# Wide broadcast of inverse denominators, small layernorm steps and an early x in a fused attention and feed-forward kernel

## The chip, the cores and the metric

The kernel runs on one core of one Trainium2 chip. The metric is the device time of one execution in microseconds (us). A run is called fast here unless it is over 1.5% above the fastest run of the same kernel; ratios use fast runs alone. Names of the engines in the profile: PE is the matrix engine, ACT the scalar engine, DVE the vector engine, POOL the general one, and SP the one that does nothing here but issue transfers. "SPq" and "ACTq" in a row mean that this engine's sequencer was busy issuing a transfer.

## The reference

```python
xn = layernorm(x)                                # x: [1, 2048, 448] bf16
# attention with a memory: 16 heads of 28, 4 segments of 512 tokens
for s in range(4):
    p     = softmax(qs @ ks.T * scale + mask)    # causal, inside the segment
    a_dot = p @ vs
    num   = phi(qs) @ M                          # M, z: what earlier segments left
    den   = phi(qs) @ z + 1e-6
    o     = g * num / den + (1 - g) * a_dot      # g = sigmoid(beta), per head
    M, z  = M + phi(ks).T @ vs, z + sum(phi(ks))
s_ = concat(o) @ wo
gate = silu((gelu(xn @ w_gate) * (xn @ w_up)) @ w_down)   # 448 -> 1792 -> 448
out = x + s_ * gate
```

## The kernel before

The heads lie in four groups (g) of four. Everything is written in program order by a scheduler of its own: attention of a segment has 24 half-steps, n0 to n23, and each half-step issues one pair of scores, its exp on ACT, its causal mask on POOL (`affine_select`), the value products of two steps earlier, and then some "filler": projections, the down product, output blocks. In the traces each engine takes up its work in program order.

Both divisions, by the softmax denominator (side 0) and by the memory denominator (side 1), take one path: a row of each head's denominators is stored to DRAM, loaded back as [128, 64], inverted by DVE, stored again, and read back in four broadcasts, one for each head group, in which the row of each of its four heads goes to 32 partitions:

```python
def evac(s, g, side, ps):
    t = oup.tile([P, L], F32, name=f"oU{side}")          # pool of 4 buffers per side
    nc.vector.tensor_copy(out=t[:], in_=ps[:])
    oU[s, g, side] = t
    nc.sync.dma_start(out=den[s][side, g * HG:(g + 1) * HG, :], in_=t[Dh:P:HP, :])

def invert(s, side):
    dc = small.tile([P, 64], F32, name="dc")
    rdr = dram.tile([H, L], F32, name="rdr")
    nc.sync.dma_start(out=dc[:], in_=den[s][side].rearrange("h (c f) -> (h c) f", f=64))
    def rest():
        ...                                              # add, gate, reciprocal on DVE
        nc.sync.dma_start(out=rdr[:].rearrange("h (c f) -> (h c) f", f=64), in_=dc[:])
        for g in range(G):
            r = rbp.tile([P, L], F32, name="rb")
            nc.sync.dma_start(
                out=r[:], in_=rdr[g * HG:(g + 1) * HG, :].unsqueeze(1).to_broadcast([HG, HP, L]))
            rb[s, g, side] = r
    later(2, rest)                                       # two half-steps later

def combine(s, g):                                       # POOL
    ...
    nc.gpsimd.tensor_tensor(out=o_a[:], in0=o_a[:], in1=r[:], op=ALU.mult)
    nc.gpsimd.tensor_tensor(out=dst, in0=o_a[:], in1=oU.pop((s, g, 1))[:], op=ALU.add)
```

An output block (four per segment) loads its x once more as `xr`, multiplies, adds on POOL and stores. The load and the store both go through SP:

```python
def fin(b):
    xr = work.tile([P, D], BF16, name="xr")
    nc.sync.dma_start(out=xr[:], in_=x_v[s][:, b, :])
    ...                                                  # oT @ wo on PE, times the gate on DVE
    nc.gpsimd.tensor_tensor(out=o_out[:], in0=t[:], in1=xr[:], op=ALU.add)
    nc.sync.dma_start(out=o_v[s][:, b, :], in_=o_out[:])
```

At the start SP loads x, ACT loads wq; POOL squares wq and wk for a guard (a check that no logit can overflow), and DVE normalizes x.

Of the kernel before, what the change touches and what calls it, by code (L numbers as in the profile page):

```python
# [17 lines left out]
P = 128  # L18
NSEG = 4
HP = 32  # L20
# [5 lines left out]
def fast_path(tc, A_x, A_wq, A_wk, A_wv, A_wo, A_beta, B_w_gate, B_w_up, B_w_down, out):  # L26
# [16 lines left out]
    with ExitStack() as ctx:  # L43
# [25 lines left out]
        def load_x(s):  # L69
            x_sb[s] = xp.tile([P, NB, D], BF16, name="x_sb")  # L70
            for b in range(0, NB, 2):
                nc.sync.dma_start(out=x_sb[s][:, b:b + 2, :], in_=x_v[s][:, b:b + 2, :])

# [7 lines left out]

        wq_raw = seg1.tile([DC, NDC, D], BF16, name="hT")
        wk_raw = const.tile([DC, NDC, D], BF16, name="wk_raw")
# [4 lines left out]
        wo_sb = const.tile([P, G, D], BF16, name="wo_sb")  # L88
        w_dma(nc.scalar, wq_raw, A_wq, DC)
        w_dma(nc.scalar, wk_raw, A_wk, DC)  # L90
# [52 lines left out]
        def tick():  # L143
# [3 lines left out]
            for _, _, fn in due:  # L147
                fn()

        def guard():  # L150
            sqs = {}
            for nm in ("wq", "wk"):
                t = oup.tile([DC, NDC, D], BF16, name="oU" + ("0" if nm == "wq" else "1"))
                nc.gpsimd.tensor_tensor(out=t[:], in0=raw[nm][:], in1=raw[nm][:], op=ALU.mult)
                sqs[nm] = t
            ones = const.tile([P, 1], BF16, name="ones")
            nc.gpsimd.memset(ones[:], 1.0)
            nrm = small.tile([1, 2, H], F32, name="nrm")
            for i, nm in enumerate(("wq", "wk")):
                np_ = ps_m.tile([P, L], F32, name="m")  # L160
                for c in range(NDC):
                    nc.tensor.matmul(out=np_[0:1, 0:D], lhsT=ones[0:DC, :], rhs=sqs[nm][:, c, :],
                                     start=(c == 0), stop=(c == NDC - 1))
                nc.vector.reduce_sum(out=nrm[:, i, :],
                                     in_=np_[0:1, 0:D].rearrange("p (h d) -> p h d", d=Dh), axis=AX.X)
# [3 lines left out]
                                    scalar2=None, op0=ALU.is_lt)  # L169
            oki = const.tile([1, 1], mybir.dt.int32, name="oki")  # L170
            nc.vector.tensor_reduce(out=oki[:], in_=okh[:], op=ALU.min, axis=AX.X)
            return oki

        xnT = {}

        def layer_norm(s):
# [6 lines left out]

            def stats(h):
                for b in (h, h + 1):
                    st = small.tile([P, nc.vector.BN_STATS_DIM], F32, name="st")
                    nc.vector.bn_stats(out=st[:], in_=xs[:, b, :])
                    nc.vector.bn_aggr(out=mv[:, b, :], in_=st[:])
                r = rstd[:, h:h + 2]
                nc.vector.tensor_scalar(out=r, in0=mv[:, h:h + 2, 1], scalar1=EPS, scalar2=None,  # L190
                                        op0=ALU.add)
                nc.gpsimd.tensor_tensor(out=r, in0=r, in1=nhalf[:, h:h + 2], op=ALU.pow)  # L192

# [16 lines left out]

            def both(*fs):
                def run():
                    for f in fs:
                        f()
                return run
            A = lambda f, *a: (lambda: f(*a))
            return [A(stats, 0), A(stats, 2), A(scale_x, 0),
                    both(A(turn, 0), A(scale_x, 1)), both(A(put, 0), A(turn, 1), A(scale_x, 2)),
                    both(A(put, 1), A(turn, 2), A(scale_x, 3)), both(A(put, 2), A(turn, 3)), A(put, 3)]

# [128 lines left out]
        def memory_read(s, g):  # L349
            np_ = ps_m.tile([P, L], F32, name="m")  # L350
            nc.tensor.matmul(out=np_[:], lhsT=mbd[:, g, :], rhs=pqT[s][:, g, :], start=True, stop=True)
            evac(s, g, 1, np_)

        rb = {}

        def invert(s, side):

            dc = small.tile([P, 64], F32, name="dc")
            rdr = dram.tile([H, L], F32, name="rdr")
            nc.sync.dma_start(out=dc[:], in_=den[s][side].rearrange("h (c f) -> (h c) f", f=64))  # L360

            def rest():
                nc.vector.tensor_scalar(out=dc[:], in0=dc[:], scalar1=(1e-6 if side else 0.0),
                                        scalar2=igate[:, side:side + 1], op0=ALU.add, op1=ALU.mult)
                nc.vector.reciprocal(out=dc[:], in_=dc[:])
                nc.sync.dma_start(out=rdr[:].rearrange("h (c f) -> (h c) f", f=64), in_=dc[:])
                for g in range(G):
                    r = rbp.tile([P, L], F32, name="rb")
                    nc.sync.dma_start(
                        out=r[:], in_=rdr[g * HG:(g + 1) * HG, :].unsqueeze(1).to_broadcast([HG, HP, L]))  # L370
                    rb[s, g, side] = r
            later(2, rest)

# [123 lines left out]

        with tc.manual_schedule():
            ln = layer_norm(0)
            ln[0]()  # L500
            pad_weight("wq")
            for f in ln[1:]:
                f()
            pad_weight("wk")
            gates()
            run(project_units(0))
            oki = guard()

            for s in range(NSEG):
                last = s == NSEG - 1  # L510

                if not last:
                    table = {}
                    if s > 0:
                        p_ = s - 1
                        in_turn(table, 0, ends)
                        in_turn(table, 2, [lambda: invert(p_, 0)])
                        in_turn(table, 9, [lambda g=g: combine(p_, g) for g in range(G)])
                    in_turn(table, 1, layer_norm(s + 1))
                    gate_up(s, table)  # L520
                if s + 2 < NSEG:
                    load_x(s + 2)
# [3 lines left out]
                if last:  # L526
                    in_turn(at, 0, ends)
                    in_turn(at, 2, [lambda: invert(s - 1, 0)])
                    in_turn(at, 8, [lambda g=g: combine(s - 1, g) for g in range(G)])
                    in_turn(at, 13, [lambda g=g: memory_read(s, g) for g in range(G)])  # L530
                    in_turn(at, 18, [lambda: invert(s, 1)])
                elif s > 0:
                    pre += [(0.22, lambda g=g: memory_read(s, g)) for g in range(G)]
                    in_turn(at, 7, [lambda s=s: invert(s, 1)])
                    in_turn(at, 14, [lambda s=s, g=g: scale_memory(s, g) for g in range(G)], 2)
                if not last:
                    pre.append((0.9, lambda s=s: update(s)))
                    lists.append(project_units(s + 1))
                if s < 2:
                    lists.append(down_units(s))  # L540
                if last:
                    lists.append(down_units(s - 1))
                    pre += merge(*lists)
                    lists = [finish_units(s - 1)]
                elif s > 0:
                    lists.append(finish_units(s - 1))
                ends = attention(s, pre + merge(*lists), at)
# [3 lines left out]
            in_turn(table, 0, ends)  # L551
            in_turn(table, 3, [lambda g=g: scale_memory(s, g) for g in range(G)])
            in_turn(table, 2, [lambda: invert(s, 0)])
# [389 lines left out]
```

## Time and profile before

| | before |
|---|---|
| median of the first three runs | 360.02 us (358.03 to 363.34) |
| span of the profile, granted clock of PE | 359.6 us, 0.916 |
| first projection on PE | 17.5 us |
| holes of PE over 2 us after that | 9.9, 13.0, 5.7, 13.1, 2.9 us |

The page's busy times (us, share of the span, number of instructions):

```profile
PE 281.8 (78%) x1619; PEld 115.5 (32%) x1620; DVE 162.5 (45%) x301; ACT 149.5 (42%) x211; POOL 139.5 (39%) x221
```

A hole is a stretch in which PE runs no matmul. PE has 78 us without work, and no other engine is half busy. So the question is not which engine has too much work, but what PE waits for at each hole, followed back. The granted clock is the share of full speed that PE was given; when it is 0.5, the texts call the clock cold or half. "Segment 1" in the prediction is attention 1 here, and so on.

### The profile page before, as it was taken

Reading aid. Unit: us, or ns where it says so; the run is one execution under the profiler, and the core shown is the slowest. Engines: PE = TensorE matmul, PEld = TensorE weight load, DVE = VectorE, ACT = ScalarE, POOL = GpSimd, SP = SyncE. Lnnn points to the kernel's source line nnn. Section 1 sums busy time; section 2 is a strip of 40 time slices with the busy share of each in tenths; the row PEclk is TensorE's granted clock in tenths of the full one; section 3 lists DMA queues with packets and bytes.
Section 4 is the critical chain, followed back from the end, with each engine's and each line's share of the span. In section 5 each row is a group of like instructions: output and inputs, shape, how many; then the busy total and the mean of one; then the engine's idle time right before and its main releaser. Section 6 shows DMA issues by size and latency. Waiting matters only on the chain. (4 is left out here: it accounts for less than half of the span.)

```text
span 359.6 us, 4459 instructions
## 1 busy us (share of the span) xinstructions
PE 281.8 (78%) x1619; PEld 115.5 (32%) x1620; DVE 162.5 (45%) x301; ACT 149.5 (42%) x211; POOL 139.5 (39%) x221
## 2 busy tenths in 40 slices
PE   0299999999999989908998988509875960599991
PEld 0234344333334433302343433102331320134450
DVE  2748754555566475602558556503311540034341
ACT  1223323866742375611652367504681750013310
POOL 6620100433310454106621567018648720452822
PEclk9999999999999999965999999856996996579998
DMA  7996000000001400121000201121112023102111
GB/s 189 262 289 130 0 1 2 0 5 1 3 5 42 129 19 16 42 93 39 9 21 9 102 20 29 59 77 39 30 39 86 7 57 106 52 17 83 52 51 48
DMA packets 17414, 20.32 MB, mean 57 GB/s; under 512 B 3064, under 2 KB 12792, under 8 KB 17384
## 3 DMA queue, kind: packets, MB, share of 16 engines
q1 hardware_dynamic: 15960, 17.55, 16.7%
q10 hardware_dynamic: 1392, 2.41, 2.6%
q8 instruction: 14, 0.23, 0.3%
q14 instruction: 16, 0.13, 0.1%
q0 software_dynamic: 32, 0.00, 0.0%
HBM read 17.66 MB, written 2.29 MB: 56 GB/s over the span
## 5 line engine op out<-in xcount | busy, mean ns | idle before, releaser
L322 ACT ACTIVATE pt<-s 128x1024 bf16<-128x1024 f32 (+1 forms) x96 | 82.3, 884 | 61.2 <-PE s L318 35.0
L325 POOL TENSOR_SCALAR_AFFINE_SELECT pt<-pt 128x256 bf16<-128x256 bf16 x128 | 51.5, 423 | 68.4 <-ACT pt L322 67.9
L400 ACT ACTIVATE gl<-s 128x512 bf16<-128x512 f32 x56 | 33.4, 597 | 91.4 <-PE s L397 87.3
L401 DVE TENSOR_TENSOR hT<-gl,s 128x512 bf16<-128x512 bf16 x56 | 38.4, 685 | 66.7 <-ACT gl L400 66.7
L397 PE MATMUL s<-xnT,wg_sb 112*128 112x512 bf16 x224 | 59.8, 391 | 1.2 <-DVE hT L401 1.2
L397 PE MATMUL s<-xnT,wu_sb 112*128 112x512 bf16 x224 | 59.3, 389 | 0.0
L335 PE MATMUL pv<-pt,vaug 128*32 128x512 bf16 (+3 forms) x256 | 21.1, 326 | 46.6 <-POOL pt L325 40.3
L412 PE MATMUL m<-wd_sb,hT 128*128 128x448 bf16 x224 | 51.6, 367 | 0.0
L441 POOL TENSOR_TENSOR o_out<-sg,xr 128x448 bf16<-128x448 f32 x16 | 16.5, 1031 | 65.6 <-DMA xr<-in_A_x_dram 47.5
L318 PE MATMUL s<-qT,kT 32*128 32x128 bf16 (+3 forms) x256 | 33.1, 311 | 2.5 <-ACT pt L322 1.8
L397 PEld LDWEIGHTS <-wu_sb 112*128 112x128 bf16 x224 | 22.3, 100 | 27.7 <-issue 2.2
L397 PEld LDWEIGHTS <-wg_sb 112*128 112x128 bf16 x224 | 21.2, 100 | 26.1 <-issue 5.3
L345 DVE COPY oU<-pv 128x512 f32<-128x512 f32 x16 | 10.9, 684 | 37.2 <-PE pv L335 28.3
L412 PEld LDWEIGHTS <-hT 128*128 128x128 bf16 x224 | 20.3, 100 | 22.3 <-issue 6.5
L335 PEld LDWEIGHTS <-vaug 128*32 128x32 bf16 x256 | 6.3, 95 | 59.7 <-issue 57.3
L192 POOL TENSOR_TENSOR rstd<-rstd,nhalf 128x2 f32<-128x2 f32 x8 | 5.9, 742 | 45.3 <-DVE rstd L190 45.3
L385 POOL TENSOR_TENSOR oU<-oU,rb 128x512 f32<-128x512 f32 x12 | 15.2, 1266 | 20.6 <-DMA rb<-rdr 20.2
L318 PEld LDWEIGHTS <-kT 32*128 32x128 bf16 x256 | 9.9, 92 | 37.4 <-issue 37.1
L202 PE MATMUL m<-ident,xn 128*112 128x128 bf16 x64 | 7.1, 249 | 17.0 <-DVE xn L196 16.7
L234 PE MATMUL m<-xnT,wq_pad 112*128 112x512 bf16 x64 | 18.3, 412 | 0.7 <-ACT xnT L207 0.7
L234 PE MATMUL m<-xnT,wk_pad 112*128 112x512 bf16 x64 | 18.4, 415 | 0.0
L421 DVE SCALAR_TENSOR_TENSOR sg<-th,m 128x448 f32<-128x448 f32 x16 | 9.8, 614 | 15.4 <-ACT th L416 13.3
(75 smaller groups left out, 289.7 us busy)
## 6 DMA issues: line engine op xcount, KB each, us to landing
rb<-rdr SPq DMA_DIRECT2D x28, 256.0 KB
x_sb<-in_A_x_dram SPq DMA_DIRECT2D x8, 224.0 KB
xr<-in_A_x_dram SPq DMA_DIRECT2D x16, 112.0 KB
out_dram<-o_out SPq DMA_DIRECT2D x16, 112.0 KB
wu_sb<-in_B_w_up_dram ACTq DMA_DIRECT2D x1, 1568.0 KB
wg_sb<-in_B_w_gate_dram SPq DMA_DIRECT2D x1, 1568.0 KB
wd_sb<-in_B_w_down_dram SPq DMA_DIRECT2D x1, 1568.0 KB
den<-oU SPq DMA_DIRECT2D x28, 8.0 KB
```

The lines of the kernel that those rows point to most:

```text
L234: nc.tensor.matmul(out=pr[:], lhsT=wpad[nm][:, c, g * HG:(g + 1) * HG, :].rearrange("p h d -> p (h d)"), rhs=xnT[s][:, c, :], start=(c == ...
L318: nc.tensor.matmul(out=sp[:, j, c0:c0 + n], lhsT=kT[s][r, g, kb * P:(kb + 1) * P], rhs=qT[s][r, g, kb * P:L], start=True, stop=True)
L322: nc.scalar.activation(out=pt[:, :, 0:w], in_=sp[:, :, 0:w], func=ACT.Exp, scale=scale)
L325: nc.gpsimd.affine_select(out=v, in_=v, pattern=[[0, 2], [1, P]], compare_op=ALU.is_ge, fill=0.0, base=0, channel_multiplier=-1)
L335: nc.tensor.matmul(out=acc[i * HP:(i + 1) * HP, kb * P:L], lhsT=va[:, kb, g * HG + i, :], rhs=pts[i // 2][:, i % 2, c0:c0 + n], start=(kb ...
L345: nc.vector.tensor_copy(out=t[:], in_=ps[:])
L385: nc.gpsimd.tensor_tensor(out=o_a[:], in0=o_a[:], in1=r[:], op=ALU.mult)
L397: nc.tensor.matmul(out=gu[:, i, :], lhsT=w_sb[:, c, fc * P:(fc + 1) * P], rhs=xnT[s][:, c, :], start=(c == 0), stop=(c == NDC - 1))
L400: nc.scalar.activation(out=gl[:], in_=gu[:, 0, :], func=ACT.Gelu_apprx_tanh)
L401: nc.vector.tensor_tensor(out=hT[s][:, fc, :], in0=gl[:], in1=gu[:, 1, :], op=ALU.mult)
L412: nc.tensor.matmul(out=d_ps[:, 0:D], lhsT=hT[s][:, fc, b * P:(b + 1) * P], rhs=wd_sb[:, fc, :], start=(fc == 0), stop=(fc == NFC - 1))
L441: nc.gpsimd.tensor_tensor(out=o_out[:], in0=t[:], in1=xr[:], op=ALU.add)
```

## The change

Its intent: the broadcast reads a source whose slowest dimension is 16 and not four, and is meant to go over 16 transfer engines; `xr`, which comes behind it, should land early. For this the inverse is written four times. Besides, layernorm is spread over more steps of gate/up, the guard's squares go from POOL to ACT, x is loaded first over both queues, and the memory reads, scalings and output blocks are laid out anew. The core of it, cut:

```diff
-                nc.sync.dma_start(out=x_sb[s][:, b:b + 2, :], in_=x_v[s][:, b:b + 2, :])
+                eng = nc.scalar if s == 0 and b else nc.sync
+                eng.dma_start(out=x_sb[s][:, b:b + 2, :], in_=x_v[s][:, b:b + 2, :])
...
-        w_dma(nc.scalar, wq_raw, A_wq, DC)
+        w_dma(nc.sync, wq_raw, A_wq, DC)
...
-                nc.gpsimd.tensor_tensor(out=t[:], in0=raw[nm][:], in1=raw[nm][:], op=ALU.mult)
+                nc.scalar.activation(out=sqs[nm][:], in_=raw[nm][:], func=ACT.Square)
...
+            if g == G - 1:                               # in memory_read
+                later(2, lambda: invert(s, 1))
+                for i in range(G):
+                    later(11 + 2 * i, lambda i=i: scale_memory(s, i))
...
-            rdr = dram.tile([H, L], F32, name="rdr")
+            rdr = dram.tile([H, 4, L], F32, name="rdr")
-                nc.sync.dma_start(out=rdr[:].rearrange("h (c f) -> (h c) f", f=64), in_=dc[:])
+                for j in range(4):
+                    nc.sync.dma_start(out=rdr[:, j, :].rearrange("h (c f) -> h c f", f=64), in_=dc[:])
-                        out=r[:], in_=rdr[g * HG:(g + 1) * HG, :].unsqueeze(1).to_broadcast([HG, HP, L]))
+                        out=r[:], in_=rdr[g * HG:(g + 1) * HG].rearrange("h j l -> (h j) l")
+                        .unsqueeze(1).to_broadcast([HG * 4, HP // 4, L]))
-            later(2, rest)
+            later(3, rest)
...
-                    in_turn(at, 8, [lambda g=g: combine(s - 1, g) for g in range(G)])
-                    in_turn(at, 13, [lambda g=g: memory_read(s, g) for g in range(G)])
-                    in_turn(at, 18, [lambda: invert(s, 1)])
+                    in_turn(at, 10, [lambda g=g: combine(s - 1, g) for g in range(G)])
+                    in_turn(at, 15, [lambda g=g: memory_read(s, g) for g in range(G)])
```

(Left out: the table of 16 small layernorm steps in place of eight, the order of layernorm 0 around the two weight copies, the guard as two steps inside gate/up 0, and a reordering of the filler.)

## The prediction

> **What bounds the kernel now.** I read the page's row of slices first, then the list of waits, then the timelines of PE, POOL and of the SP queue around each hole in PE, and last the first 20 us.
>
> The page's slices, 9 us each:
>
> ```profile
> PE   0299999999999989908998988509875960599991
> PEclk9999999999999999965999999856996996579998
> DMA  7996000000001400121000201121112023102111
> ```
>
> PE is 9 or 8 nearly everywhere, so this is a TensorE-bound kernel with holes, and each hole comes with a fall of the granted clock. The timeline of PE gives the resumptions (columns: start us, duration us, engine, line, operation, tiles; in brackets the idle time before and what ended it):
>
> ```profile
> 162.84 0.76 PE L335 MATMUL pv<-pt,vaug 128*32 128x256 bf16 x4 [9.91 <-POOL pt L325]
> ...
> 242.46 0.76 PE L335 MATMUL pv<-pt,vaug 128*32 128x256 bf16 x4 [13.03 <-POOL pt L325]
> ...
> 273.79 0.62 PE L335 MATMUL pv<-pt,vaug 128*32 128x512 bf16 x4 [5.72 <-DVE oU L345]
> ...
> 307.67 0.65 PE L335 MATMUL pv<-pt,vaug 128*32 128x384 bf16 x6 [13.14 <-POOL pt L325]
> ...
> 315.09 0.40 PE L335 MATMUL pv<-pt,vaug 128*32 128x256 bf16 x2 [2.91 <-POOL pt L325]
> ```
>
> Five holes, 44.7 us in all: one in attention segment 1, one in segment 2, three in segment 3 (the last two at its end, where gate/up of segment 3 already begins). The mask (POOL, L325) is late. The list of waits says what held POOL:
>
> ```profile
> POOL o_out L441 <- DMA xr<-in_A_x_dram: 47.5, 10, 15.3
> PE pv L335 <- POOL pt L325: 40.3, 6, 13.1
> POOL oU L385 <- DMA rb<-rdr: 20.2, 3, 10.0
> ```
>
> POOL runs in order, and sits before the final add (L441) for the 112 KB of x (xr), with the masks queued behind. Why xr is late is seen in the SP queue and POOL of segment 1:
>
> ```profile
> 147.82 2.44 SPq L369 DMA_DIRECT2D rb<-rdr  x4
> 150.31 1.73 SPq L433 DMA_DIRECT2D xr<-in_A_x_dram  x1
> ```
>
> ```profile
> 161.40 1.03 POOL L441 TENSOR_TENSOR o_out<-sg,xr 128x448 bf16<-128x448 f32 x1 [14.79 <-DMA xr<-in_A_x_dram]
> ```
>
> xr is issued right after four broadcasts of 256 KB and lands 11 us later; undisturbed it takes about 2 us (the chain of waits has "2.04 DMA xr" and 2.11 in segment 3). In between the stretches view shows a quarter of the DMA engines busy:
>
> ```profile
> 155.00:157.00 2.00, 0.00 (x0) 0.00 (x0) 0.00 (x0) 0.00 (x0) 0.00 (x0) 0.74 0.26 98
> 157.00:159.00 2.00, 0.00 (x0) 0.00 (x0) 0.00 (x0) 0.00 (x0) 0.00 (x0) 0.50 0.26 99
> ```
>
> (Last columns: clock, DMA share, GB/s.) 0.26 of 16 engines is four; 1.05 MB at 99 GB/s is 10.6 us. The start is bounded by something else:
>
> ```profile
> 9.67 0.63 DVE L187 BATCH_NORM_STATS2 st<-x_sb 128x6 f32<-128x448 bf16 x1 [1.80 <-DMA x_sb<-in_A_x_dram]
> ...
> 12.26 3.17 POOL L154 TENSOR_TENSOR oU<-hT 112x1792 bf16<-112x1792 bf16 x1
> ...
> 12.57 3.34 DVE L196 TENSOR_SCALAR xn<-x_sb,mv,rstd 128x448 bf16<-128x448 bf16 x2 [0.53 <-PE m L202]
> ...
> 17.51 1.87 PE L234 MATMUL m<-xnT,wq_pad 112*128 112x512 bf16 x4 [0.73 <-ACT xnT L207]
> ```
>
> The second half of x lands at 9.7, and two scalings that should take 0.39 each take 3.34 while POOL squares the weight. PE really starts at 17.5.
>
> [...] four matmuls of 448 columns took 1.67 us until about 169, then 0.93. [...]
>
> **The change part by part.** I wrote out the order in which each half-step of attention (24 per segment, n0 to n23) issues its work, and took durations from the rows above.
>
> *Broadcast over 16 engines.* 64 KB per engine and DMA become 16 KB. At the 280 GB/s of the first 25 us (page: 262, 289 in slices 1 and 2) 1.05 MB takes 3.7 us instead of 10.6. Added: three more writes of 32 KB at about 0.35 us of SP issue each, so 1.1 us per inversion; the four broadcasts still cost 2.44 us of issue. So xr behind a broadcast lands some 4 us after its issue, not 11.
> Segment 1: the broadcasts (emitted at n5) leave SP at about n10.6 (half-step 1.6 us), xr lands at n12.6, while POOL needs it at n10. In the kernel before POOL stood still from 146.6 and PE only from 152.9: 6 us of slack. The wait is now 4 us, so PE loses about 0.5. Before: 9.9 hole, and 162.84 to 169.5 at half clock, 3.3 more. Gain 12.7.
> Segment 2: half-steps of 1.3 us, broadcasts at n7, xr wanted at n9 and there at n13.7: 5 to 6 us against 6 of slack, PE loses 1. Before 13.0 and 242.46 to 248.2 cold (2.8). Gain 14.8.
> Segment 3, first hole: the evacuation of head group 0 needs the buffer that the first combine frees. Before, that waited for rb until 270.41. rb will be there, but the combine is moved from n8 to n10, behind the exp (0.5) and the mask (0.41) of n10, then 2 x 1.26 of combine and 0.69 of evacuation: 4.5 us remain[...]. Before 5.7 + 2.6. Gain 2.3.
> Segment 3, last holes: four final adds come at n18, n20, n21, n22, and now ahead of the broadcasts. But SP alternates load and store, and each store waits for its add: 2.1 landing + 1.03 add + 0.34 + 0.44 issues, with gaps about 3.7 us per block (the same spacing as at 306.23, 309.88, 313.65 in POOL before). With the last memory read also at n18 the first xr lands 5 us after n18, so the adds end at 6.1, 10.4, 14.3, 18.2 us after n18. PE reaches the products that need the masks behind the last three at 9.0, 13.4 and 15 us (waits shifting those after it): 2.3 + 1.4 + 3.7 = 7.4 us of waiting, perhaps 1.5 cold. Before 16.0 + 8.5/2 = 4.2 cold. Gain 11.3.
>
> *End.* The memory inversion of segment 3 now follows those adds, and the rb buffers (4) must be given back by the scaling before the next four broadcasts. With 1.27 per scaling and 2.53 per combine the last combine ends at about 43.9 us after n18, and PE wants it at 41.9. Loss 2.0. Before, the last combine ended at 340.6, just before PE's use at 340.95.
>
> *Layernorm in small steps.* Gate/up takes 26.8 us in segment 0 (35.1 to 61.9), 27.8 in 1 and 2; 112 matmuls at 0.216 and 16 transposes make 25.2, with the leftover products 25.8. DVE per step is 0.69 + 0.76 = 1.45 under PE's 1.73, so most vanishes: 1.2 + 1.3 + 1.3. Against it, the two squares on ACT (1792 columns at ACT's 1024 in 0.884 us: 1.6 each) delay one gelu: 0.7. Gain 3.1.
> *Guard's PE work* (1.67) moves but stays: 0.
> *Memory reads spread.* At 126.5 and 210.4 PE loses 1.2 and 1.4 to evacuation; gain 1.6.
>
> *Start.* x comes 4 us earlier, and POOL no longer blocks DVE. But wq goes from first on ACT's queue to second on SP's, and DVE copies wq before the statistics of block 2. By queue, SP had moved 0.24 MB at 5 us and 0.40 at 7, then only 0.06 per us while ACT carried wu in large packets:
>
> ```profile
> q10 hardware_dynamic: 123, 0.44, 80.8%
> q1 hardware_dynamic: 123, 0.11, 24.0%
> ```
>
> (9 to 11 us; q10 is ACT.) wu now starts about 1.2 us earlier, so SP's 0.63 MB (half of x, wq) is complete at about 11 and usable at 12.4. Then 0.62 copy, two statistics, scalings, wk copy, pow and the last transpose: about 18.2 instead of 17.5. Loss 0.7.
>
> Sum: 12.7 + 14.8 + 2.3 + 11.3 - 2.0 + 3.1 + 1.6 - 0.7 = 43.1; 360.0 - 43.1 = 317.
>
> **Rivals.** (a) The broadcast goes wide but not fast, or the extra writes and SP's issue time take its place: then xr still lands 7 to 8 us late, segments 1 and 2 keep 2 to 3 us each with cold clocks: about 327. For it: SP is blocked 2.4 us in any case. Against: the loads at the start use all 16 at 240 to 340 GB/s. (b) All PE holes vanish: 334.6 us of PE span less 44.7, 12.9 cold, 5.5 layernorm and some 4 of small gaps, plus 20 us of start and tail, is 288. Against: the buffer wait in segment 3 and the serial adds are untouched. Half-way gives about 305. (c) PE holes go but POOL becomes the bound: it has 139.5 us of work, in segment 3 10 us of combines in a row; that is already in my numbers. (d) The start goes better: if wq lands by 9, it gains 4 instead of losing 0.7: 312.
>
> **Range and chances.** The two middle holes (27 of 43 us) are the surest. The end of segment 3 and the tail are uncertain by 6 us, the start by 3, the rest by 3: 306 to 327. No path to a loss is visible: faster 0.97, same 0.02, slower 0.01.
>
> **What would show it.** Right: DMA share near 1 for under 4 us after each broadcast; the 9.9 and 13.0 us holes under 2 us; clock 1.0 through segments 1 and 2; a hole of 4 to 5 us before head group 1's products in segment 3; some 7 us of mask waits at its end; DVE waiting for wq until about 12. Wrong: holes of over 4 us behind xr in segments 1 and 2; PE starting before 15; no wait on the first combine; the final output products waiting for nothing.

Where a cut is marked, rules were taken out that no trace of this case shows, and with them one term of the sum: 1.5 us of cold clock that the author expected after the first hole of segment 3. The sum came to 43.1 with this term in it: the gain of 2.3 there is 5.7 + 2.6 - 4.5 - 1.5, and the terms that still stand give 3.8 there and 44.6 in all. The 1.5 us cold at the last holes stays as the author's estimate, against the 4.2 read from the trace of before. Three things that the forecast takes as given, with what the traces show: the broadcast on 4 engines and then on 16 is a DMA share of 0.26 in before and of 1.02 in after (the second was an expectation when it was written); the loads at the start on all 16 are shares of 0.96, 1.12 and 1.10 in the three microseconds from 3 to 6 us of before; ACT's 0.884 us is the page's mean over two shapes, and 128x1024 alone took 1.025. The time of the matmuls of 448 columns belongs to the cold stretch after the hole of 9.91 in before.

## The result, and the profile after

| | before | after |
|---|---|---|
| median (lowest to highest), four runs each | 359.47 (358.03 to 363.34) | 332.78 (330.94 to 333.58) |
| span of the profile, granted clock | 359.6, 0.916 | 331.6, 0.951 |

The ratio is 0.9235, with a 95% interval of 0.9151 to 0.9319. A ratio is the mean time of one kernel's fast runs over that of the other's from the same rounds, so it is not quite the ratio of the medians quoted. The result is correct against the reference. The kernel became faster, but by 27 us and not by 43; 332.8 lies outside the range of 306 to 327.

The page after: busy times, and the slices of PE and its clock (8.3 us each):

```profile
PE 279.2 (84%) x1620; PEld 116.1 (35%) x1620; DVE 159.5 (48%) x301; ACT 152.0 (46%) x213; POOL 132.9 (40%) x219
...
PE   0699989999999999989999998198837973979691
...
PEclk9999999999999999999999999659996997799898
```

PE's work is the same 280 us; the span lost 28 us of waiting. The middle of the row is now full, where there was one hole of 9.9 us; two deep holes are left, in the slices of 207 to 216 and of 240 to 249 us, and a ragged end. The timeline of PE names them (in brackets the idle time before, and what ended it):

```profile
146.83 0.29 PE L354 MATMUL pv<-pt,vaug 128*32 128x256 bf16 x2 [0.86 <-POOL pt L344]
...
214.57 0.76 PE L354 MATMUL pv<-pt,vaug 128*32 128x256 bf16 x4 [6.72 <-POOL pt L344]
...
250.44 0.62 PE L354 MATMUL pv<-pt,vaug 128*32 128x512 bf16 x4 [7.03 <-DVE oU L364]
...
280.53 0.40 PE L354 MATMUL pv<-pt,vaug 128*32 128x256 bf16 x2 [3.96 <-POOL pt L344]
...
293.79 1.02 PE L422 MATMUL s<-xnT,wg_sb 112*128 112x512 bf16 x4 [1.96 <-DVE hT L426]
...
312.45 0.46 PE L461 MATMUL m<-wo_sb,oT 128*128 128x448 bf16 x1 [2.19 <-POOL oT L411]
```

The first row answers the hole of 9.91 before, the second that of 13.03, the third that of 5.72, the fourth those of 13.14 and 2.91 (three smaller waits of 0.90, 1.10 and 1.16 us for the same masks stand ahead of it). The last two are new. POOL's two longest waits for a transfer are still the same (us in total, number of waits, longest):

```profile
POOL o_out L466 <- DMA xr<-in_A_x_dram: 31.4, 10, 9.6
...
POOL oU L410 <- DMA rb<-rdr: 19.6, 3, 9.3
```

The wait for xr fell from 47.5 to 31.4 us in ten waits: less, but far from gone, though the broadcast ahead of it is now wide. To compare sum by sum with the prediction, the span is cut at the first matmul of each stage on PE (attention 3 at the first down product of its filler, 257.06 and 231.24 us, which is 2.1 and 0.6 us after its first scores):

| stage | before | after | change | predicted |
|---|---|---|---|---|
| start to first projection | 17.5 | 13.8 | -3.7 | +0.7 |
| projections and gate/up 0 | 44.4 | 44.2 | -0.2 | -0.5 |
| attention 0 | 36.8 | 36.8 | 0 | 0 |
| gate/up 1 and 2 | 55.6 | 51.9 | -3.7 | -2.6 |
| attention 1 | 56.1 | 42.6 | -13.6 | -13.5 |
| attention 2 | 46.6 | 42.0 | -4.6 | -15.6 |
| attention 3 | 35.3 | 38.2 | +2.9 | -2.3 |
| gate/up 3, with the last mask waits | 45.9 | 36.4 | -9.5 | -11.3 |
| down 3 and tail | 21.3 | 25.7 | +4.4 | +2.0 |
| sum | 359.5 | 331.6 | -28.0 | -43.1 |

(The prediction's parts are put into stages by where they lie; the gain from the memory reads is split between attention 1 and 2. The rows are rounded, so a sum can miss its span or its column by 0.1.) Attention 2 is 11 us short of its prediction, attention 3 five (cut at its first scores, 12.5 and 3.7). The start gained what was not predicted.

Attention 2 in detail, first SP's queue:

```profile
201.02 2.51 SPq L390 DMA_DIRECT2D rdr<-dc  x4
...
206.28 2.48 SPq L393 DMA_DIRECT2D rb<-rdr  x4
208.80 0.55 SPq L366 DMA_DIRECT2D den<-oU  x1
209.39 0.44 SPq L458 DMA_DIRECT2D xr<-in_A_x_dram  x1
```

Four writes take 2.51 us to issue; SP then stands until they have landed (206.28), issues four broadcasts for 2.48, a store for 0.55, and only then, 8.4 us after the first write, the one load that POOL waits for. Next, three views: DVE where it takes up this inversion; POOL at the add behind this load and at the first combine of attention 3; and the stretch of 208 to 210 us (its length, then the busy time of PE, PE's weight loads, DVE, ACT and POOL; the row ends with the clock, the DMA share and GB/s):

```profile
200.16 0.25 DVE L386 TENSOR_SCALAR dc<-dc,igate 128x64 f32<-128x64 f32 x1
```

```profile
213.13 1.03 POOL L466 TENSOR_TENSOR o_out<-sg,xr 128x448 bf16<-128x448 f32 x1 [9.59 <-DMA xr<-in_A_x_dram]
...
247.06 1.26 POOL L410 TENSOR_TENSOR oU<-oU,rb 128x512 f32<-128x512 f32 x1 [1.90 <-DMA rb<-rdr]
```

```profile
208.00:210.00 2.00, 0.00 (x0) 0.00 (x0) 0.08 (x1) 1.24 (x2) 0.00 (x0) 1.00 1.02 276
```

The broadcast itself does what it should: all 16 engines (share 1.02) at 276 GB/s, against 0.26 and 98 before. xr lands 3.7 us after its issue, as predicted (4). It is late because it is issued late. POOL stands from 203.54, PE from 207.85, 4.3 us later.

### The profile page after: what moved, and what is told of

Same layout as the page of the kernel before. It is cut to its first block, busy times and chain, and to the rows that moved or that the text cites. A ratio compares the mean times of both kernels' runs of the same rounds, so it can differ in the third digit from the quotient of the medians.

```text
span 331.6 us, 4480 instructions
## 1 busy us (share of the span) xinstructions
PE 279.2 (84%) x1620; PEld 116.1 (35%) x1620; DVE 159.5 (48%) x301; ACT 152.0 (46%) x213; POOL 132.9 (40%) x219
## 3 DMA queue, kind: packets, MB, share of 16 engines
q1 hardware_dynamic: 19512, 18.41, 21.3%
## 4 chain that ended last, share of the span: by engine, by line
PE 54%; DMA 16%; POOL 11%; SPq 6%; DVE 5%; ACT 3%; issue 3%; POOLq 0%; DVEq 0%; ACTq 0%
PE s L422 21%; PE m L253 8%; PE m L437 7%; DMA xr<-in_A_x_dram 6%; PE s L337 5%; PE m L275 3%; DMA rdr<-dc 3%; POOL o_out L466 3%; POOL oU L410 3%; PE pv L354 3%; POOL oT L411 3%; PE m L283 3%; SPq L390 2%; SPq L393 2%; DMA oT<-in_A_wq_dram 2%
## 5 line engine op out<-in xcount | busy, mean ns | idle before, releaser
L422 PE MATMUL s<-xnT,wg_sb 112*128 112x512 bf16 x224 | 58.9, 386 | 3.3 <-DVE hT L426 3.3
L422 PE MATMUL s<-xnT,wu_sb 112*128 112x512 bf16 x224 | 58.4, 384 | 0.0
L337 PE MATMUL s<-qT,kT 32*128 32x128 bf16 (+3 forms) x256 | 33.1, 309 | 2.5 <-ACT pt L341 2.3
L466 POOL TENSOR_TENSOR o_out<-sg,xr 128x448 bf16<-128x448 f32 x16 | 16.9, 1059 | 41.0 <-DMA xr<-in_A_x_dram 31.4
L253 PE MATMUL m<-xnT,wq_pad 112*128 112x512 bf16 x64 | 19.1, 427 | 0.7 <-ACT xnT L209 0.7
L461 PE MATMUL m<-wo_sb,oT 128*128 128x448 bf16 x64 | 16.0, 369 | 3.0 <-POOL oT L411 3.0
```

The costliest lines, as they stand in the source:

```text
L253: nc.tensor.matmul(out=pr[:], lhsT=wpad[nm][:, c, g * HG:(g + 1) * HG, :].rearrange("p h d -> p (h d)"), rhs=xnT[s][:, c, :], start=(c == ...
L337: nc.tensor.matmul(out=sp[:, j, c0:c0 + n], lhsT=kT[s][r, g, kb * P:(kb + 1) * P], rhs=qT[s][r, g, kb * P:L], start=True, stop=True)
L422: nc.tensor.matmul(out=gu[:, i, :], lhsT=w_sb[:, c, fc * P:(fc + 1) * P], rhs=xnT[s][:, c, :], start=(c == 0), stop=(c == NDC - 1))
L461: nc.tensor.matmul(out=a_ps[:, 0:D], lhsT=oT[s][:, g, b * P:(b + 1) * P], rhs=wo_sb[:, g, :], start=(g == 0), stop=(g == G - 1))
```

## The experiments

Two theories stand against each other. The **chain theory**, named in the expectations from the first run on, says that what holds POOL is xr's place in SP's queue: behind a serial chain (cast, inversion on DVE, writes, their landing, broadcasts), of which the width shortens one link. The **width theory** is the prediction's: xr is late because of the bytes ahead of it, and is early once they go over 16 engines. The first two runs set the chain theory against another rival, that the remaining parts of the change carry the gain; order and bytes are set against each other from two_copies on, and most directly by xr_on_act and before_xr_on_act. Each kernel was timed beside the kernel before on the same chip, in three or five rounds. Unless another base is named, the edit is made on the kernel after. Four of the profiles (wide_alone, narrow_back, six_buffers, squares_on_pool) fell on runs called slow; their waits and stages are read as hints, and their times are taken from the fast runs.

### wide_alone and narrow_back: the broadcast on its own, and all without it

wide_alone is the kernel before with only the four writes and the wide broadcast:

```diff
+            rdr = dram.tile([H, 4, L], F32, name="rdr")
+                for j in range(4):
+                    nc.sync.dma_start(out=rdr[:, j, :].rearrange("h (c f) -> h c f", f=64), in_=dc[:])
+                        out=r[:], in_=rdr[g * HG:(g + 1) * HG].rearrange("h j l -> (h j) l")
+                        .unsqueeze(1).to_broadcast([HG * 4, HP // 4, L]))
```

> The kernel before with the broadcast over 16 engines alone (four copies written, nothing else moved). Theory of the SP chain (the holes that remain come from POOL standing in order before an add whose x is late, because SP issues it behind inversion, four writes, four broadcasts): the hole of segment 1 goes from 9.9 us to under 2, that of segment 2 from 13.0 to 5 to 8, the last ones shrink from 16.0 to about 8; 333 to 345 us. Rival (the gain of the whole change comes mostly from start, layernorm steps and memory reads): over 350 us.

narrow_back is the reverse of these lines in the kernel after.

> The changed kernel with the broadcast put back on 4 engines (one copy). Chain theory: xr lands 9 to 11 us after its issue again, holes of 10 us or more return in segments 1 and 2, 350 to 362 us. Rival (the other parts carry the gain): under 342 us.

wide_alone: 347.72 us (344.51 to 350.78), ratio 0.9534 (0.9427 to 0.9640). narrow_back: 346.42 us (342.38 to 347.74), ratio 0.9544 (0.9432 to 0.9656). Each half gives about six tenths of what the whole gives (0.9235), so the two overlap, and neither number lies where one theory alone had put it. The large hole of attention 2, in wide_alone and then in narrow_back:

```profile
230.07 0.76 PE L335 MATMUL pv<-pt,vaug 128*32 128x256 bf16 x4 [8.63 <-POOL pt L325]
```

```profile
223.37 0.76 PE L354 MATMUL pv<-pt,vaug 128*32 128x256 bf16 x4 [9.73 <-POOL pt L344]
```

The width alone takes the hole from 13.0 to 8.6, the new order alone to 9.7, both to 6.7. In attention 1 both leave 4.6 of 9.9, and only together they leave 0.9. So the width is worth something, but the prediction gave it nearly the whole of both holes.

### x_resident: no xr at all

All four x tiles stay in SBUF and the add reads them there. The room comes from the guard's squares, which go into other buffers.

```diff
-        xp = pool("xp", 2)
+        xp = pool("xp", 4)
-                xr = work.tile([P, D], BF16, name="xr")
-                nc.sync.dma_start(out=xr[:], in_=x_v[s][:, b, :])
-                nc.gpsimd.tensor_tensor(out=o_out[:], in0=t[:], in1=xr[:], op=ALU.add)
+                nc.gpsimd.tensor_tensor(out=o_out[:], in0=t[:], in1=x_sb[s][:, b, :], op=ALU.add)
```

> The changed kernel with all four segments of x kept in SBUF, so that the final add waits for no load (and, to make room, the squares of the guard go into other tiles). Chain theory: the hole of segment 2 (6.7 us and 4.5 us of cold clock) and the mask waits at the end of segment 3 (about 7.9 us in all and 2 us cold) go, and the tail loses its load-store alternation: 309 to 317 us; the first hole of segment 3 (7.0) stays. Rival (POOL has too much work, masks are late anyhow): holes of over 4 us stay at these places, over 325 us.

311.46 us (310.79 to 312.28), ratio 0.8622 (0.8550 to 0.8694); clock 0.969. At the place of the hole of 6.72 PE no longer waits for a mask (the longest wait in attention 2 is one of 0.92 for DVE, elsewhere), attention 2 takes 32.0 us (after: 42.0; the prediction had come to 31.0), gate/up 3 31.6 (36.4). The first hole of attention 3 stays at 6.69. So xr explains 10 of the 11 us that attention 2 missed, and the miss of gate/up 3, and does not explain the first hole of attention 3. It does not yet tell whether it was xr's order or its bytes.

### xr_on_act: the same loads, issued by the other queue

```diff
-                nc.sync.dma_start(out=xr[:], in_=x_v[s][:, b, :])
+                nc.scalar.dma_start(out=xr[:], in_=x_v[s][:, b, :])
```

> The changed kernel with the loads of x for the final add issued by ACT instead of SP, nothing else. If SP's order makes the load late (it is issued 5 to 6 us after PE's own unit, behind writes and broadcasts), the hole of segment 2 (6.7 us) falls under 2.5 us and the mask waits at the end of segment 3 shrink: 316 to 326 us. If the bytes of the broadcast on the same engines are in its way, the hole stays over 4 us and the time at 328 or more.

312.26 us (311.66 to 313.96), ratio 0.8712 (0.8658 to 0.8766). One word gives nearly all that removing the loads gave, and more than was expected (316 to 326). Two of the issues on ACT, the writes on SP, and the wait of POOL in this kernel:

```profile
199.45 0.33 ACTq L458 DMA_DIRECT2D xr<-in_A_x_dram  x1
205.21 0.34 ACTq L458 DMA_DIRECT2D xr<-in_A_x_dram  x1
```

```profile
199.94 2.50 SPq L390 DMA_DIRECT2D rdr<-dc  x4
```

```profile
POOL o_out L466 <- DMA xr<-in_A_x_dram: 10.4, 6, 3.1
```

The first of the four loads, which SP had issued at 209.39, leaves ACT at 199.45, ahead of SP's first write (199.94 in this kernel, which is 1.1 us earlier at this place). Its add runs at 202.43 and not at 213.13. The second leaves while the broadcasts are being issued (205.15 to 207.63), and its add runs at 207.82. The wait falls from 31.4 to 10.4 us and attention 2 is 32.2 us long. The bytes are the same and the broadcast is the same: the place in SP's queue was the cause. For the first load this place holds both, SP's waiting and the bytes ahead; the second load, which goes out while the broadcasts are being issued and still causes no wait (its add starts 2.6 us after the issue), suggests that the bytes alone do little. Stage by stage the last four stages now take 32.2 + 36.1 + 32.1 + 22.3 = 122.7 us. The prediction's 31.0 + 33.0 + 34.6 + 23.3 makes 121.9, and the kernel after took 142.3. The expected gain had gone into the place of these loads. (The parts agree less well than the sum, which is in part luck: the first hole of attention 3 stays, at 6.90.)

### before_xr_on_act: the one word in the kernel before

The same edit, on the kernel before, with its narrow broadcasts.

> The kernel before with the loads of x for the final add issued by ACT, the broadcast narrow as it was. If the bytes of the narrow broadcast on four engines make the load late, the holes of segments 1 and 2 stay over 5 us each: 345 us or more. If it is SP's order, they fall under 3 us each, and so do those at the end of segment 3: 320 to 335 us.

325.90 us (325.23 to 326.45), ratio 0.9027 (0.8973 to 0.9082), on a chip where the kernel before took 361.51. The ratio's interval lies wholly below that of the entire change (0.9151 to 0.9319), although the two were measured on different chips, each against the kernel before. Attention 1 takes 43.2 us (56.1 before), attention 2 34.1 (46.6), with no change of the broadcast. This is the strongest evidence against the prediction's sizing. In the trace the two queues move at the same time: a load of xr was issued by ACT at 217.00, while narrow broadcasts issued from 214.29 to 216.73 were still moving. By queue (packets, MB, share of 16 engines), from 219 to 220 us:

```profile
q1 hardware_dynamic: 156, 0.19, 51.3%
q10 hardware_dynamic: 94, 0.07, 29.6%
```

q10 (ACT) moves 0.07 of xr's 0.11 MB in this microsecond, while SP's q1 still carries the broadcast, and a store of 112 KB; all of xr is in by 223. In the kernel before, on SP's queue, it took 11 us. So the delay of 11 us was seen behind the broadcast on SP's own queue, and here, on a second queue, all of the load was in within 6 us. What is left in this kernel is the hole of attention 3 that waits for a buffer (5.84 us) and one of 11.61, with its cause:

```profile
281.27 0.40 PE L335 MATMUL pv<-pt,vaug 128*32 128x256 bf16 x2 [11.61 <-POOL pt L325]
```

```profile
POOL o_out L441 <- DMA out_dram<-o_out: 12.2, 1, 12.2
```

Here the add waits 12.2 us for its output buffer: the earlier store sits on SP behind narrow broadcasts. So SP's order passes the delay on to a store as well. In xr_on_act, with the wide broadcast and the rest of the change, PE has no wait of 0.8 us or more for a mask; that the width alone does this was not tested.

### narrow_x_resident: what the width is worth without xr

x_resident with the one write and the four-engine broadcast.

> x kept in SBUF, but the broadcast on 4 engines with one copy. If the width gains only by way of the load of x, the time is within 3 us of the kernel with x kept and wide broadcast (309 to 314). If the scalings and combines need the width too (they wait on POOL for the same broadcasts), it is 5 us or more slower: 316 to 330.

313.98 us (313.19 to 315.33), ratio 0.8764 (0.8714 to 0.8813), against 0.8622 for the wide one on another chip: 1.6%, with intervals that just miss each other; by the medians 2.5 us. Attention 2 takes 33.1 us (wide: 32.0), gate/up 3 34.9 (31.6), there with a wait of PE for DVE of 8.23 us (4.33), since the chain behind it is longer. So with xr out of the way the wide broadcast is worth some 2.5 to 5 us of 360 (by medians and by ratios, on different chips); the time lies at the upper edge of what was expected if the width gains only by way of xr (309 to 314), and most of what it gives in wide_alone comes through xr.

### two_copies and two_queues: shortening the four writes

two_copies writes the inverse twice and broadcasts from a source whose slowest dimension is 8 (its DMA share was not read); two_queues gives half of the four writes to ACT.

```diff
+            rdr = dram.tile([H, 2, L], F32, name="rdr")            # two_copies
+                for j in range(2):
+                        .unsqueeze(1).to_broadcast([HG * 2, HP // 2, L]))
...
-                    nc.sync.dma_start(...)                          # two_queues, in the write loop
+                    (nc.sync, nc.scalar)[j % 2].dma_start(...)
```

> The changed kernel with two copies written instead of four[...]. If the issue time of the writes on SP (0.63 us each, 2.5 us for four) is what the chain lacks, two writes save 1.25 us per inversion while the transfer grows by at most 2 us: within 2 us of the changed kernel, or faster (328 to 334). If the width of the transfer is what counts, the hole of segment 2 grows by 2 us or more and the time goes over 336.

> The changed kernel with two of the four writes issued by ACT instead of SP. Chain theory: xr in segment 2 and the first broadcast of segment 3 come 1.25 us earlier, holes shrink by about 1 us each: 328 to 332 us. Rival (ACT's own queue is in order and its exp and gelu wait behind those issues): the same or slower, 333 to 338.

two_copies: 332.22 us (330.43 to 333.32), ratio 0.9225 (0.9153 to 0.9296), the same as after. SP and POOL of it:

```profile
206.84 0.52 SPq L458 DMA_DIRECT2D xr<-in_A_x_dram  x1
```

```profile
213.33 1.03 POOL L466 TENSOR_TENSOR o_out<-sg,xr 128x448 bf16<-128x448 f32 x1 [9.76 <-DMA xr<-in_A_x_dram]
```

xr is issued 2.6 us earlier than at 209.39, and its add starts 0.2 us later: what two writes less save in issue and landing (about 1.3 us each) is lost again behind the broadcast from two copies (from xr's issue to its add 6.5 us, and 3.7 in the kernel after). So on one queue both count, order and bytes. two_queues: 336.05 us (333.70 to 337.90), ratio 0.9323 (0.9245 to 0.9401). The hole of attention 2 falls to 4.10, but gate/up 1 grows from 25.9 to 29.7 us, gate/up 2 to 27.8. The author's reading is that the writes wait on ACT for DVE's inversion and hold up what stands behind them: before one gelu ACT is idle for 3.5 us, but the list of waits puts this down to PE, so it is not shown. In this kernel a load without inputs could go to a compute engine's queue at no visible cost (0.33 us of issue each on ACT); with the writes, which must wait for another engine, the stage became 3.8 us longer.

### combine_at_8 and six_buffers: the first hole of attention 3

The prediction had this hole come from moving the combines from n8 to n10. (six_buffers also moves the guard's squares into other tiles, to make room.)

```diff
-                    in_turn(at, 10, [lambda g=g: combine(s - 1, g) for g in range(G)])
+                    in_turn(at, 8, [lambda g=g: combine(s - 1, g) for g in range(G)])     # combine_at_8
-            t = oup.tile([P, L], F32, name=f"oU{side}")
+            t = oup.tile([P, L], F32, name=f"oU{side}", bufs=4 + 2 * (1 - side))          # six_buffers
```

> The changed kernel with the four combines of segment 3 put back from half-step 10 to 8. If, as the prediction had it, the place of the combine behind the exp and mask of half-step 10 makes the first hole of segment 3, the hole (7.0 us) shrinks by 2 us or more and the time by 2 to 4 us. If the late landing of the broadcast sets it (the first combine waits 1.9 us for it in the changed kernel), the hole stays between 6 and 7.5 us and the time within 2 us of the changed kernel.

> The changed kernel with six instead of four buffers for the attention numerators (guard squares moved to make room). If the first hole of segment 3 (7.0 us, then 2.3 us of cold clock) is a wait for the buffer that the first combine frees, it goes and the time falls by 6 to 10 us, to 323 to 327. Rival (the combines' 10 us on POOL hold the masks in any case): PE waits for POOL's mask there instead, and the gain is under 4 us, over 329.

combine_at_8: 334.56 us (331.39 to 335.04), ratio 0.9277 (0.9190 to 0.9364); hole 7.10, unchanged. Its first combine:

```profile
247.63 1.26 POOL L410 TENSOR_TENSOR oU<-oU,rb 128x512 f32<-128x512 f32 x1 [3.68 <-DMA rb<-rdr]
```

It starts at 247.63 instead of 247.06, however early it is placed; it only waits longer for rb (3.68 against 1.90). So the late broadcast sets the hole, not the place of the combine: the prediction's "rb will be there" is refuted. Two runs made for another purpose agree: where SP issues only two of the writes, this hole is 5.72 (two_copies) and 4.52 (two_queues). six_buffers: 333.06 us (327.78 to 335.54), where three of four runs are called slow, so no ratio is given and its time is inconclusive. Its waits say something: the hole of 7.03 for a buffer turns into two waits of 2.39 and 2.41 for the mask, with attention 3 at 34.3 us instead of 38.2, while attention 2 takes 45.1 and the tail 29.0 (42.0 and 25.7 in the kernel after). The buffer was the wait that ended last; POOL's row of combines ahead of the masks stood close behind it.

### ln_old_steps, queues_back and squares_on_pool: the smaller parts

```diff
+            for n, f, b in ((1, stats, 0), (1, stats, 1), (2, stats, 2), (2, stats, 3), ...    # ln_old_steps: before's eight steps
...
+                eng = nc.sync                             # queues_back
+        w_dma(nc.scalar, wq_raw, A_wq, DC)
...
+                nc.gpsimd.tensor_tensor(out=sqs[nm][:], in0=raw[nm][:], in1=raw[nm][:], op=ALU.mult)
+                next(check)                               # squares_on_pool: squared at the start again
```

> The changed kernel with the layernorm work put back into the steps of gate/up where the kernel before had it (two statistics in a step, one block after another). If the small steps give what the stages show, gate/up of segments 1 and 2 goes from 25.9 back to 27.8 us each and the time grows by 3 to 5 us; in segment 0 it stays at 28.4 or grows by up to 1. Rival (the stages lost DVE time for another reason): gate/up stays at 26.

> The changed kernel with the first x on SP's queue only and the weight wq first on ACT's queue, as before. If the two queues make the earlier start (projections at 13.8 us instead of 17.5), projections start at 15 to 16 us and the time grows by 1 to 2.5 us. If it is POOL's squares being gone that makes it, they start at 14.5 or before and the time stays within 1 us.

> The changed kernel with the two squares of the guard on POOL at the start, as before, instead of on ACT inside gate/up. If POOL blocking DVE made the late start, the scalings of blocks 2 and 3 take 3 us instead of 0.70, projections start at 16 us, but the 1.4 us wait of PE in gate/up of segment 0 goes: net +0.5 to +1.5 us. If the start came from the queues: projections within 0.5 us of 13.8, and net -1 us.

ln_old_steps: 337.32 us (334.36 to 340.69), ratio 0.9325 (0.9231 to 0.9420). Gate/up 1 and 2 take 27.8 us each again, gate/up 0 29.3 (28.4). The 4.7 us that this makes is what the three small holes were predicted to give (1.2 + 1.3 + 1.3), and somewhat more.

queues_back: 333.88 us (331.48 to 338.13), ratio 0.9273 (0.9206 to 0.9341). The projections start at 12.5 us, not later than at 13.8. So which queue carries x first did not make the earlier start; the time grew by 1.1 us, which the intervals do not tell from nothing.

squares_on_pool: 336.50 us (334.41 to 339.46), ratio 0.9335 (0.9275 to 0.9395). The projections start at 18.7. DVE and POOL at that time:

```profile
10.88 6.41 DVE L198 TENSOR_SCALAR xn<-x_sb,mv,rstd 128x448 bf16<-128x448 bf16 x2
```

```profile
10.79 3.17 POOL L157 TENSOR_TENSOR oU<-oT 112x1792 bf16<-112x1792 bf16 x1
13.92 3.20 POOL L157 TENSOR_TENSOR oU<-wk_raw 112x1792 bf16<-112x1792 bf16 x1
```

Two scalings that take 0.70 us in the kernel after end at 17.29, just after the two multiplications (17.12). POOL started first (10.79 against 10.88), and each scaling ends 0.1 to 0.2 us after one of POOL's multiplications: the second at 17.29, and PE takes up the first at 14.15, where the first multiplication ends at 13.96. So each scaling lasted as long as the multiplication beside it; why is not shown. As a whole this costs about 3.6 us, more than was expected (0.5 to 1.5).

### combined, combined_dve_add and six_rb: a better version

combined is x_resident with six buffers and the last inversion's second half six steps after its load instead of three. combined_dve_add makes the final add on DVE. six_rb is combined with six buffers for rb and four steps instead of six.

```diff
+        xp = pool("xp", 4)                                # and no xr, as in x_resident
+            t = oup.tile([P, L], F32, name=f"oU{side}", bufs=4 + 2 * (1 - side))
+            later(6 if s == NSEG - 1 and side == 0 else 3, rest)
-                nc.gpsimd.tensor_tensor(out=o_out[:], in0=t[:], in1=x_sb[s][:, b, :], op=ALU.add)
+                nc.vector.tensor_tensor(out=o_out[:], in0=t[:], in1=x_sb[s][:, b, :], op=ALU.add)   # combined_dve_add
+        rbp = pool("rbp", 6)                              # six_rb
```

> x kept in SBUF, six numerator buffers, and the last inversion taken up three steps later, so that DVE does not stand before its denominators (4.3 us wait of PE in gate/up of segment 3 with x kept). If these waits add up, 300 to 307 us: 311.5 less about 4 for the first hole of segment 3 and 4 for the DVE wait. If the waits only move (POOL masks in segment 3, combines at the end), 308 to 313.

> The same with the final add of x on DVE instead of POOL (16 x 1.03 us off POOL, some 16 x 0.65 us onto DVE). If POOL's order holds the masks in segment 3, 1 to 4 us faster than the combined kernel, 297 to 305. If DVE's work is then in the way of the evacuations, the same or slower.

> The combined kernel with six instead of four broadcast buffers, and the last inversion one step later instead of three. If the last combines wait for buffers that the scalings give back, the 6.9 us that PE waits for them at the end falls to under 4 and the time to 303 to 307 us. If it is the chain of SP and POOL before them, the wait stays and the time is within 2 us of 309.4.

combined: 309.44 us (308.49 to 312.43), ratio 0.8621 (0.8539 to 0.8704). combined_dve_add: 309.90 us (306.99 to 312.34), 0.8569 (0.8477 to 0.8661). six_rb: 310.17 us (309.00 to 310.41), 0.8634 (0.8587 to 0.8681). They cannot be told apart from each other or from x_resident (0.8622) by their intervals. In combined the wait of gate/up 3 is gone (25.0 us, from 31.6 in x_resident), but down 3 takes 30.3 us (22.8), with waits of 1.3, 3.41 and 2.2 us for the last combines. In six_rb the end waits 4.3 us, gate/up 3 again has a wait of 2.9, and attention 3 has two, of 2.55 and 2.40. So the wait is moved and not removed; why is not tested. By the program, the last softmax inversion and the eight POOL instructions of its combines can't start before attention 3 has ended.

Left open: a broadcast over 16 engines from one copy would need no extra writes. No run here has one, so what 16 engines give with a single write was not measured.

## Why the prediction was right or wrong, point by point

- **Broadcast in attention 1: right in size.** 13.5 predicted for the stage (12.7 for the hole and half of the memory reads), 13.6 measured; hole 0.86 (predicted 0.5), POOL's wait for xr 4.29 (predicted 4). But the number does not belong to the width alone: wide_alone and narrow_back each leave 4.6 us of this hole, and before_xr_on_act gains 12.9 without it.
- **Broadcast in attention 2: wrong, and the largest failure (11 us).** The step is "xr wanted at n9 and there at n13.7: 5 to 6 us against 6 of slack, PE loses 1". In microseconds that was 8.7 after n7 (6.7 half-steps of 1.3). Measured: n7's projection is at 198.48 on PE and xr lands at about 213.0, 14.5 later. What was mis-sized is the time from n7 to the issue of xr: 10.9 us, and not 4.7. SP's first write could start only 2.5 us after n7, as DVE took up the inversion at 200.16, behind a cast; four writes took 2.51 us to issue, 0.63 each, and not 0.35 (the duration of the single [128, 64] write of before, 0.32, was taken for one of another shape); they landed 2.75 after that; a denominator store of 0.55 was not counted. The prediction names no time for DVE's part and for the landing: its 8.7, less 1.4 for the writes, 2.4 for the broadcasts and 4 for xr, leaves 0.9 us for both. The broadcast's 2.48 and xr's own 3.7 were as predicted. And the slack was 4.3, not 6. The 6 had been read at attention 1; at attention 2 the trace of before shows 3.7 (POOL stands from 225.73, PE from 229.43), which the prediction overlooked. The hole is 6.72, and the clock stayed at half until about 223.9, another 4 to 5 us of loss. xr_on_act and x_resident, with 32.2 and 32.0 us for the stage, show that xr's lateness is 10 of these 11 us.
- **Size of the width as such: too large.** The prediction saw "1.05 MB at 99 GB/s is 10.6 us" and gave the bytes the whole delay. narrow_x_resident puts the width at 2.5 to 5 us where xr is out of the way; before_xr_on_act reaches 0.9027 without it.
- **First hole of attention 3: wrong in cause and size (5.2 us for the stage).** "rb will be there" failed: rb was issued at 243.49 to 246.0, after four writes from 239.57 to 242.07, and the first combine waited until 247.06. combine_at_8 shows that the placement, to which the prediction gave the hole, has no effect. 7.03 instead of 4.5, and about 4 us at a cold clock (0.5 from 250.44 to 254.56).
- **Last mask waits: right in kind and sum.** 7.4 us were predicted from the serial chain of load, add and store; 0.90 + 1.10 + 1.16 + 3.96 make 7.1. The split was not the predicted one (2.3, 1.4, 3.7), so the closeness is in part luck. Gate/up 3 then has a wait of 1.96 for DVE, which stood 2.62 us in order before a load of denominators; this was not in the sum, and the stage gained 9.5 and not 11.3.
- **End: right in kind, low in size.** 2.0 predicted; PE waits 0.83 + 2.19, and then works at a cold clock (14 matmuls in 4.44 us, the next 14 in 2.81): 4.4 for the stage.
- **Layernorm steps: right, and somewhat low in size.** -3.7 in gate/up 1 and 2 (predicted -2.6), confirmed by ln_old_steps. In gate/up 0 the two squares on ACT (1.69 us each, predicted 1.6) made a hole of 1.39 (0.7), and that stage grew from 26.8 to 28.4 us.
- **Start: wrong, in the good direction.** The step is "SP's 0.63 MB (half of x, wq) is complete at about 11 and usable at 12.4". DVE copied wq at 7.96:

```profile
7.96 0.63 DVE L113 COPY wq_pad<-oT 112x1792 bf16<-112x1792 bf16 x1 [1.96 <-DMA oT<-in_A_wq_dram]
```

  The prediction had taken the two queues' shares of bandwidth from one trace of the start. These shares are not a property of the queues: wide_alone, with the start of the kernel before, began its projections at 14.8, before_xr_on_act at 17.0, the kernel before at 17.5, by when x's second half came. Rival (d), "if wq lands by 9, it gains 4", is what happened. Of the 3.7 us about 2.6 (an estimate) is the scalings' freedom from POOL's squares (3.34 against 0.70 us); the rest is within what arrival varies.
- **Rivals.** (a), xr still some us late with cold clocks and 327 us, was closest in mechanism: it named the extra writes and SP's issue time. It was given too little weight, and put the loss into attention 1 and 2 alike, where only 2 had it. Two of the prediction's own signs of being wrong came true: a hole of over 4 us behind xr (6.72, in segment 2 alone), and PE starting before 15 (13.8).

## What to carry to other kernels

Before a transfer is widened, read the issuing queue: what stands ahead of the load that is late, and whether it stands there for bytes, for issue time, or for a wait of its own; then try the one-word move of that load to another queue first, which here gave more (0.9027) than the whole change (0.9235). Slack is to be read at the place itself: the 6 us taken over from attention 1 were 3.7 at attention 2 before and 4.3 after, and a wait put at 1 us became a hole of 6.7, with 4 to 5 us at half clock behind it. An engine that serves two masters in program order (POOL: final adds and masks) passed the delay of the unimportant one on to the important one.

## What else the traces of this case show

- Order on a queue: moving 16 loads of 112 KB from SP to ACT took the kernel from 361.5 to 325.9 us, since on SP they stood behind transfers that wait for other engines, and behind their bytes. The other half: with half of four dependent writes moved to ACT, gate/up 1 was 3.8 us longer.
- Issue time by access pattern: SP took 0.63 us for a write of [16, 8, 64] to DRAM (0.60 for the first of the four, with nothing just ahead of it) and 0.32 for the same bytes as [128, 64]; four of them were 2.51 us on the path.
- Recovery of the clock: after the hole that ended at 214.57 four matmuls of 512 columns took 1.89 us at 217.62 and 1.26 still at 223.34, and 1.04 from 224.85: some 9 us, with PE busy nearly all the time. After two later holes of the same run the full clock was back after 4.1 us (250.44 to 254.56) and 4.8 (280.53 to 285.28).
- POOL beside DVE: two scalings went from 0.70 to 6.41 us beside two POOL multiplications of 3.17 and 3.20.
